# Feed-forward weights in 25 pieces, softmax by halves of heads in one-chain steps, and the first segment's sorted values copied tile to tile

## Chip, cores and metric

The kernel runs on one core of a Trainium2 chip. The metric is the device time of one execution in microseconds; smaller is better. The kernel before has a median of 1527.66 us over 3 runs (1521.85 to 1530.99).

## What is computed

x has 2048 rows of 448 numbers (bf16). Two kinds of layer alternate, A B A B, each added to its input:

```
x = x + A(layernorm(x));  x = x + B(layernorm(x));  x = x + A(layernorm(x));  x = x + B(layernorm(x))

A: mem = mem0                                     # 8 rows
   for each segment s of 32 rows (64 of them):
       h = concat(mem, x[s])                      # 40 rows
       q, k, v = h Wq, h Wk, h Wv                 # 16 heads of 256
       p = softmax(mask(q k^T / 16));  o = (p v) Wo
       mem = o[:8];  out[s] = o[8:]               # mem goes on to the next segment
B: ((gate * (gate > 0)) * up) W_down,  gate = x W_gate, up = x W_up      # 448 -> 1792 -> 448
```

The 64 segments of a layer A form a chain, since each needs the memory rows of the one before.

## The kernel before, in words

**Weights first.** The setup multiplies Wk with Wq per head into `M_sb`/`MT_sb`, and Wv with Wo into `B_sb`/`BT_sb` (lines 602 and 611), from transposed loads on SP's queue (line 584). So a segment needs no q, k or o of its own: scores are h M h^T, and "values" are h B, 448 wide for every head.

**69 steps.** The loop at line 706 runs steps g = 0 to 68. The first layer A is chain C1 (segments 0 to 63 in steps 0 to 63), the second is chain C2, five steps later (steps 5 to 68). Steps 0 to 4 hold C1 alone, steps 64 to 68 hold C2 alone (40 rows in use, "one-chain steps"); steps 5 to 63 hold both. The order on each engine is the order in which the Python code records it; nothing is moved afterwards. Each engine works in that order, and waits are on semaphores.

**One step** (`step`, line 451):

1. `project` (lines 396 to 439): G = h M, matmuls of lines 415 and 425, copied out of PSUM by ACT and DVE at line 435 (`G`, and the last slices into `GT`).
2. Scores `S_ps` (line 486), ten matmuls, two PSUM banks of eight heads each; all G matmuls of both banks come first, then those that need `GT`.
3. Softmax: maximum (line 492) and difference (494) on DVE, exp (496) on ACT.
4. `values` (line 302), 112 matmuls of line 314 into four banks `vps` in 14 slots of 8; the banks go to `VM` by line 332 after slots 10 and 13 (second bank on DVE, the others on ACT in the first chain). `between` is the rest of the softmax (lines 507, 508, 504: sum, reciprocal, `Px` for the 32 segment rows, `Pp` for the 8 memory rows), recorded behind the copies of slot 10. The matmuls of slots 8 and 11 wait for a no-op on SP that waits for the other row half's matmuls (lines 316 to 320), so what stands on SP's queue ahead of that no-op delays PE.
5. `PT`: the weights are transposed on PE (529, 532) and copied by ACT (530) and DVE (533).
6. `AT_ps` (545): the new rows, the memory rows among them; DVE and ACT copy these into `hTr` (552 to 554), and the next step's `project` begins.

At named places between these parts (G0, G4, G9, S, V, P, B, T), the plan of lines 710 to 779 puts other work: layer norms, feed-forward matmuls (`fill`), and `warm(8)`, eight matmuls without use (line 297), at V of steps 2 and 3.

**Values for four segments at once.** The first 8 rows of a segment's x make values `VX` by `first_values`, for four segments together (step 0, at V of step 1, and each fourth step). AT needs them sorted by head, `VP`. In general `pack` (line 355) writes VX to DRAM (`VD`) and reads it back sorted, two DMAs on SP. For the first four segments `pack_first` (line 360) uses 16 DMAs of 28 KB: segment 0 by four on ACT's queue (recorded ahead of step 0's `VM` copies), segments 1 to 3 by twelve on SP's.

**Feed-forward weights** come after setup has left their place free: `ffn_weights` (line 679) issues on SP at the end of step 0 four tiles of x in one DMA, W_gate (1344 KB) and its last 64 rows (224 KB); at the end of step 1 the same of W_up; at the end of step 2 W_down (1568 KB). They are first used in step 4. SP has no other work, so "at the end of a step" means behind the no-ops of that step's `values`.

**PSUM.** `bank()` hands out six banks in turn (line 75); a separate pair `ps2` holds one of the `gps`, then S_ps, then AT_ps.

Of the kernel before, what the change touches and what calls it, by code (L numbers as in the profile page):

```python
# [18 lines left out]
H = 16  # L19
# [6 lines left out]
F = 1792  # L26
# [17 lines left out]
def build_kernel(ctx, tc, A_x, A_mem0, A_Wq, A_Wk, A_Wv, A_Wo, B_W_gate, B_W_up, B_W_down, out,  # L44
# [30 lines left out]
    def bank(shape, dt, name):  # L75

        n_bank[0] += 1
        return psum.tile(shape, dt, tag=f"b{n_bank[0] % 6}", name=name)
# [207 lines left out]
    def fill(cid, n):  # L286

        for _ in range(n):
            if ffn_q[cid]:
                fn, a, b = ffn_q[cid].popleft()  # L290
                fn(a, b)
# [60 lines left out]
    p_dram = ctx.enter_context(tc.tile_pool(name="p_dram", bufs=1, space=bass.MemoryType.DRAM))  # L352
    VD = [p_dram.tile([4, P, DM], BF, name=f"VD{i}") for i in range(2)]

    def pack(c):

        nc.sync.dma_start(VD[c.cid][:, :, :].rearrange("g p d -> p g d"), VX[c.cid][:])
        nc.sync.dma_start(VP[c.cid][:], VD[c.cid][:, :, :].rearrange("g (q s) d -> (g q) s d", s=4))

    def pack_first(eng, segments):  # L360

        for k in segments:
            for g4 in range(4):
                eng.dma_start(VP[0][32 * g4:32 * g4 + 32, k, :], VX[0][k:P:4, g4, :])

    def score_tile(h, kind, m):
        return 28 * h + (7 * m + 3 if kind else 7 * (m // 6) + m % 6 + (m % 6 > 2))
# [83 lines left out]
    def step(g, plan):  # L451

        chains = [c for c in (C1, C2) if 0 <= g - c.lag < nseg]
        both = len(chains) == 2
        rg = g % NR
        c0, c1 = chains[0].cid, chains[-1].cid + 1
        NP = L * (c1 - c0)
        r_lo, r_hi = RB2 * c0, RB2 * (c1 - 1) + L
        RR = slice(r_lo, r_hi)
        nr = r_hi - r_lo  # L460
        hT = hTr[:, rg]

        def at_place(name):
            for f in plan.get(name, []):
                f()

        for _ in range(len(deferred)):
            deferred.popleft()()
        if g == 0:
            G = G_first  # L470
        else:
            G = p_vo.tile([P, 2, 24, 2, L], BF, tag="G", name="G")
            settle()
            project(G, hT, c0, c1, at_place)

        S_ps = psum.tile([P, 2, 512], F32, tag="ps2", name="S_ps")
        wide = {c.cid: RB2 if both and c is C1 else L for c in chains}
        for last in range(2):
            for bb in range(2):
                for c in chains:  # L480
                    w = wide[c.cid]
                    o = S_ps[c.rb:c.rb + w, bb, 0:8 * L]
                    o2 = o.rearrange("p (r e k) -> p r e k", e=2, k=L)
                    for sl in (3, 4) if last else (0, 1, 2):
                        rhs = GT[:, sl - 3, 4 * bb:4 * bb + 4, c.cid, :] if last else G[:, bb, sl:24:3, c.cid, :]
                        nc.tensor.matmul(o2[:, :, sl - 3, :] if last else o, hT[:, sl].rearrange("p c t -> p (c t)")[:, L * c.cid:L * c.cid + w], rhs,  # L486
                                         start=(sl == 0), stop=(sl > 2), tile_position=(0, c.rb),
                                         skip_group_check=True)

        S3 = S_ps[RR, :, 0:8 * L].rearrange("p b (h k) -> p b h k", k=L)  # L490
        mx = p_soft.tile([P, 2, 8], F32, tag="mx")
        nc.vector.tensor_reduce(mx[RR], S3, axis=AX.X, op=ALU.max)
        se = p_soft.tile([P, H, L], F32, tag="se")
        nc.vector.tensor_tensor(se[RR].rearrange("p (b h) k -> p b h k", b=2), S3,  # L494
                                mx[RR].unsqueeze(3).to_broadcast([nr, 2, 8, L]), op=ALU.subtract)
        nc.scalar.activation(se[RR], se[RR], AF.Exp, scale=SCALE)  # L496
        at_place("S")
        ssum = p_soft.tile([P, H], F32, tag="ssum")
        rs = p_soft.tile([P, H], F32, tag="rs")
        Px = p_soft.tile([P, H, SEG], BF, tag="Px")  # L500
        Pp = p_soft.tile([P, H, XB], BF, tag="Pp")

        def weigh(eng, dst, lo, hi):
            eng.tensor_tensor(dst, se[RR, :, lo:hi], rs[RR, :].unsqueeze(2).to_broadcast([nr, H, hi - lo]), op=ALU.mult)  # L504

        def weights():
            nc.vector.tensor_reduce(ssum[RR, :], se[RR], axis=AX.X, op=ALU.add)  # L507
            nc.vector.reciprocal(rs[RR, :], ssum[RR, :])  # L508
            weigh(nc.vector, Px[RR], XB, L)
            weigh(nc.gpsimd if both else nc.vector, Pp[RR], 0, XB)  # L510

        if g == 0:
            lean[0] = 4
            value_weights(weights)
            first_values(C1)
            pack_first(nc.scalar, (0,))
        for c in chains:
            first = c is chains[0]
            values(lambda rows, sl: hT[rows, sl, c.cid, XB:L], VM[c.cid], [cp_a, cp_v, cp_a, cp_a if first else cp_v],
                   weights if first and g else lambda: None)  # L520
            if first:
                at_place("V")
        if g == 0:
            pack_first(nc.sync, (1, 2, 3))

        PT = p_soft.tile([P, 5, RB2 + L], BF, tag="PT")
        PT_ps = bank([P, 4, P], BF, "PT_ps")
        for g4 in range(4):
            nc.tensor.transpose(PT_ps[:, g4, RR], Px[RR, 4 * g4:4 * g4 + 4, :], ident[RR, RR])  # L529
        cp_a(PT[:, 0:4, RR], PT_ps[:, :, RR])  # L530
        PP_ps = bank([P, P], BF, "PP_ps")
        nc.tensor.transpose(PP_ps[:, RR], Pp[RR, :, :], ident[RR, RR])
        cp_v(PT[:, 4, RR], PP_ps[:, RR])
        at_place("P")
        settle()

        at2 = psum.tile([P, 2, 512], F32, tag="ps2", name="AT_ps")
        at = at2[:, 0, 0:8 * L].rearrange("p (k c t) -> p k c t", c=2, t=L)
        order = (0, 1, 4, 2, 3)
        for k in order:  # L540
            for kd in range(4):
                lo = min(128 * kd, DM - 128)
                for c in chains:
                    w = VM[c.cid][:, k, :] if k < 4 else VP[c.cid][:, (g - c.lag) % 4, :]
                    nc.tensor.matmul(at[:, kd, c.cid, :], w[:, lo:lo + 128], PT[:, k, c.rb:c.rb + L],  # L545
                                     start=(k == order[0] and kd == 0 and c is chains[0]), stop=(k == order[-1]),
                                     skip_group_check=True)
        nxt = [c for c in chains if g + 1 - c.lag < nseg]
        if nxt:
            n = slice(nxt[0].cid, nxt[-1].cid + 1)  # L550
            dst = hTr[:, (g + 1) % NR, :, n, SEG:L]
            nc.vector.tensor_copy(dst[0:64, 3], at[64:128, 3, n, SEG:L])  # L552
            nc.scalar.copy(dst[64:128, 4], at[64:128, 3, n, SEG:L])
            nc.vector.tensor_copy(dst[:, 0:3], at[:, 0:3, n, SEG:L])
        for c in chains:
            j = (g - c.lag) % 4
            (cp_a if c is C1 else cp_v)(OT[c.cid][:, :, 32 * j:32 * j + 32], at[:, :, c.cid, 0:SEG])
        at_place("B")
        settle()
        at_place("T")  # L560
        if g < 3:
            ffn_weights(g)

    bp_cm = tc.tile_pool(name="bpre", bufs=1)
    bp = bp_cm.__enter__()
# [110 lines left out]
            if i == 0:  # L676
                load_vo(3)

    def ffn_weights(g):

        if g == 0:
            bp_cm.__exit__(None, None, None)
            pw = ctx.enter_context(tc.tile_pool(name="pw", bufs=1))
            Wg["pool"] = ctx.enter_context(tc.tile_pool(name="p_fb", bufs=2))
            Wg["main"] = pw.tile([P, 3, 2, F], BF, name="Wgu")
            Wg["tail"] = pw.tile([P, F], BF, name="WguT")
            if R > 2:
                nc.sync.dma_start(x_ring[:, 2:R, :], x_dram[256:R * 128].rearrange("(t p) d -> p t d", p=P))
        if g == 2:
            nc.sync.dma_start(Wd_sb[:], B_W_down.rearrange("(f p) d -> p f d", p=P))  # L690
        else:
            w = (B_W_gate, B_W_up)[g]
            nc.sync.dma_start(Wg["main"][:, :, g, :], w[0:384].rearrange("(k p) n -> p k n", p=P))
            nc.sync.dma_start(Wg["tail"][64 * g:64 * g + 64, :], w[384:448])

    mps = transposed(mem0n, MEM)
    nc.vector.tensor_copy(mem0T[:, 0:4], mps[:, 0:4, 0:MEM])
# [8 lines left out]
    for g in range(nsteps):  # L706
# [5 lines left out]

        def put(place, f):
            plan.setdefault(place, []).append(f)

        def norm_at(key, t, first, second, n=P):
            put(first, lambda: hold.__setitem__(key, Norm(xsl(t)[0:n], n)))
# [56 lines left out]
            put("G9", lambda: prep_x(C1, gb + 2, transposed(hold["c1"], P)))  # L774
        if r:
            if not LAG <= g < nseg:
                put("V", lambda: fill(1, 4 if r < 3 else 3) if ffn_q[1] else warm(8) if r > 1 or gb else None)
            for place, n in (("P", (2, 2, 1) if g > nseg else (2, 2, 4)), ("B", (0, 0, 2) if g > nseg else (2, 2, 2))):
                put(place, lambda n=n[r - 1]: fill(1, n))
        step(g, plan)  # L780
# [81 lines left out]
```

## Time and profile before

| | |
|---|---|
| median of 3 runs | 1527.66 us (1521.85 to 1530.99) |
| the profiled execution: time / span | 1520.82 us / 1519.0 us |
| busy, share of the span: PE, DVE, ACT, POOL | 98%, 61%, 42%, 7% |
| steps, from the chain of waits: 1 / 2 / 3 | 83.2 to 100.6 / to 116.0 / to 129.9 us |
| steps 65 to 68 begin | 1447.4, 1462.1, 1476.1, 1491.7 us |
| DMA queue q1 (the kernel's own) / q8 (instructions) | 51.96 MB / 5.44 MB in 332 packets |

The span runs from the first to the last instruction; the execution's time is 1.8 us longer. The chain of waits goes back from the last instruction, at each step to what released it: it says which work set the time. In it "issue" is time in which the engine waited for nothing that the profile shows. `SPq` and `ACTq` are the queues from which DMAs are issued; q1 carries those of SP, q10 those of ACT, and q8 has 16 KB packets, PE's instructions (256 of 64 bytes; 332 of them are the 85,000 of PE).

### The profile page before, as it was taken

The page shows a single profiled execution, that of the slowest core. Times are in us where ns is not written, and L with a number is a line of the kernel's source. Part 1 is how long each engine was busy: PE and PEld are TensorE (multiplying, and loading weights), DVE is VectorE, ACT ScalarE, POOL GpSimd, SP SyncE. Part 2 cuts the span into 40 slices and gives each one's busy share as a digit, 9 for nine tenths or more (in the row PEclk, how much of TensorE's full clock was granted, in tenths as well). Part 3 has the DMA queues.
Part 4 walks back from the last instruction along what each step waited for, and adds up shares of the span by engine and source line. Part 5 has one row for each costly group of instructions (what it writes and reads, how often), then busy time and mean ns, then how long its engine had stood idle before and what let it go on. Part 6 is the DMA issues. An engine that isn't in the chain of part 4 may idle for free.

```text
span 1519.0 us, 89892 instructions
## 1 busy us (share of the span) xinstructions
PE 1483.8 (98%) x42503; PEld 1170.9 (77%) x42503; DVE 924.0 (61%) x1892; ACT 634.7 (42%) x1411; POOL 112.2 (7%) x227
## 2 busy tenths in 40 slices
PE   7989999999999999999999999999999999999998
PEld 4567777878787887878788787878778787878776
DVE  6745556666566655656666666656666665556655
ACT  4633444434344443434444343434444343434333
POOL 1000001000000000000000000000000000000000
PEclk9999999999999999999999999999999999999999
DMA  9831000000000101000010100000010000000000
GB/s 197 198 118 64 28 28 29 28 31 19 30 20 27 35 28 34 28 31 7 28 35 28 34 28 31 19 30 20 28 35 28 31 28 31 5 28 31 4 31 9
DMA packets 77122, 57.84 MB, mean 38 GB/s; under 512 B 45512, under 2 KB 71888, under 8 KB 76752
## 3 DMA queue, kind: packets, MB, share of 16 engines
q1 hardware_dynamic: 76544, 51.96, 12.1%
q8 instruction: 332, 5.44, 1.5%
q14 instruction: 38, 0.31, 0.1%
q10 hardware_dynamic: 208, 0.12, 0.0%
HBM read 24.55 MB, written 16.06 MB: 27 GB/s over the span
## 4 chain that ended last, share of the span: by engine, by line
PE 96%; DVE 2%; issue 1%; ACT 1%; POOL 0%; DMA 0%; DVEq 0%; ACTq 0%; POOLq 0%
PE vps L314 29%; PE gps L425 27%; PE gu L224 7%; PE S_ps L486 6%; PE dps L264 6%; PE gps L415 5%; PE gu L252 4%; PE AT_ps L545 4%; PE wps L611 2%; PE wps L602 2%; PE PT_ps L529 1%; PE tps L144 1%; PE gu L244 1%; PE ops L447 1%; DVE ssum L507 0%
## 5 line engine op out<-in xcount | busy, mean ns | idle before, releaser
L425 PE MATMUL gps<-hTr,M_sb 128*128 128x80 bf16 (+1 forms) x11424 | 425.3, 200 | 2.4 <-issue 2.3
L425 PEld LDWEIGHTS <-M_sb 128*128 128x128 bf16 x11424 | 404.9, 100 | 11.0 <-issue 2.7
L314 PE MATMUL vps<-B_sb,hTr 64*32 64x448 bf16 x12288 | 355.6, 350 | 0.1
L314 PEld LDWEIGHTS <-hTr 64*32 64x32 bf16 x14336 | 204.0, 93 | 130.5 <-issue 8.7
L435 DVE CAST G<-gps 128x480 bf16<-128x480 f32 (+1 forms) x272 | 168.4, 619 | 187.2 <-PE gps L425 96.3
L435 ACT CAST G<-gps 128x480 bf16<-128x480 f32 (+1 forms) x272 | 144.6, 532 | 267.7 <-PE gps L425 261.8
L332 ACT CAST VM<-vps 128x448 bf16<-128x448 f32 x325 | 161.2, 531 | 144.5 <-PE vps L314 138.8
L332 DVE CAST VM<-vps 128x448 bf16<-128x448 f32 x187 | 113.4, 624 | 73.4 <-PE vps L314 73.4
L224 PE MATMUL gu<-xnT,Wgu 128*128 128x128 bf16 (+1 forms) x1548 | 125.2, 218 | 0.0
L496 ACT ACTIVATE se<-se 104x640 f32<-104x640 f32 (+1 forms) x69 | 50.9, 737 | 157.7 <-DVE se L494 157.7
L224 PE MATMUL gu<-xnT,WguT 128*128 128x128 bf16 (+2 forms) x516 | 111.3, 218 | 0.0
L224 PEld LDWEIGHTS <-Wgu 128*128 128x128 bf16 x1548 | 104.6, 98 | 1.7 <-issue 1.5
L504 POOL TENSOR_TENSOR Pp<-se,rs 104x128 bf16<-104x128 f32 x59 | 48.1, 816 | 732.2 <-DVE rs L508 698.2
L314 PE MATMUL vps<-BT_sb,hTr 64*32 64x448 bf16 x2048 | 96.9, 349 | 0.2 <-issue 0.2
L415 PE MATMUL gps<-hTr,MT_sb 64*128 64x80 bf16 (+1 forms) x3808 | 91.5, 197 | 4.7 <-DVE hTr L552 3.1
L314 PE MATMUL vps<-B_sb,hX 64*32 64x448 bf16 x3072 | 89.8, 350 | 4.8 <-DVE hX L153 2.6
L264 PE MATMUL dps<-Wd_sb,hh 128*128 128x448 bf16 (+1 forms) x448 | 90.7, 353 | 0.0
L415 PEld LDWEIGHTS <-MT_sb 64*128 64x128 bf16 x3808 | 74.0, 97 | 20.6 <-issue 9.7
L230 DVE SCALAR_TENSOR_TENSOR hh<-gu,ut 128x256 bf16<-128x256 f32 (+1 forms) x129 | 53.7, 418 | 53.0 <-ACT ut L229 48.9
L314 PEld LDWEIGHTS <-hX 64*32 64x32 bf16 x3584 | 52.6, 92 | 36.8 <-issue 5.2
L486 PEld LDWEIGHTS <-hTr 128*40 128x40 bf16 (+1 forms) x1280 | 66.2, 104 | 18.6 <-issue 0.3
L545 PE MATMUL AT_ps<-PT,VM 128*128 128x40 bf16 x2048 | 72.4, 179 | 6.6 <-ACT PT L530 6.6
(108 smaller groups left out, 1684.6 us busy)
## 6 DMA issues: line engine op xcount, KB each, us to landing
VD<-VX SPq DMA_DIRECT2D x31, 448.0 KB, 3.1
VP<-VD SPq DMA_DIRECT2D x31, 448.0 KB, 3.1
wvo<-in_A_Wo_dram SPq DMA_DIRECT2D x2, 896.0 KB, 6.1
out_dram<-x_ring SPq DMA_DIRECT2D x15, 112.0 KB, 2.1
Wd_sb<-in_B_W_down_dram SPq DMA_DIRECT2D x1, 1568.0 KB
x_ring<-in_A_x_dram SPq DMA_DIRECT2D x12, 112.0 KB, 2.2
Wgu<-in_B_W_gate_dram SPq DMA_DIRECT2D x1, 1344.0 KB, 7.6
Wgu<-in_B_W_up_dram SPq DMA_DIRECT2D x1, 1344.0 KB, 6.3
```

The source lines that it names most:

```text
L224: nc.tensor.matmul(ps[:, i, ff], w, self.xnT[:, kd if kd < 3 else 3 + i], start=(kd == 0), stop=(kd == 3))
L230: nc.vector.scalar_tensor_tensor(out=self.hh[:, f:f + 2, :], in0=ps[:, 0], scalar=0.0, in1=ut[:, 0:2, 0:self.n], op0=ALU.max, op1=ALU.mult)
L252: nc.tensor.matmul(ps[i][:, ff], Wg["main"][:, kd, i, (f + ff) * 128:(f + ff) * 128 + 128], self.xnT[:, kd], start=False, stop=(kd == 2), ...
L264: nc.tensor.matmul(self.dps[0:self.n, 0:DM], self.hh[:, f, :], Wd_sb[:, f, :], start=(f == 0), stop=(f == FT - 1))
L314: mm = nc.tensor.matmul(ps[g4][32 * hq:32 * hq + 32, 0:DM], lhsT(rows, i if i < 3 else 3 + r), w, start=first, stop=final, tile_position=( ...
L332: evac[g4](dst[:, g4, :], ps[g4][:, 0:DM])
L415: nc.tensor.matmul(ps[h, b][:, i * NP:(i + 1) * NP], MT_sb[rows, t * 128:(t + 1) * 128], hT[rows, 3 + h, c0:c1, :], start=(i == 0), stop=F ...
L425: nc.tensor.matmul(ps[h, b][:, i * NP:(i + 1) * NP], M_sb[:, kd, t * 128:(t + 1) * 128], hT[:, kd, c0:c1, :], start=False, stop=(kd == 2), ...
L435: cp(o, src)
L486: nc.tensor.matmul(o2[:, :, sl - 3, :] if last else o, hT[:, sl].rearrange("p c t -> p (c t)")[:, L * c.cid:L * c.cid + w], rhs, start=(sl ...
L496: nc.scalar.activation(se[RR], se[RR], AF.Exp, scale=SCALE)
L545: nc.tensor.matmul(at[:, kd, c.cid, :], w[:, lo:lo + 128], PT[:, k, c.rb:c.rb + L], start=(k == order[0] and kd == 0 and c is chains[0]), ...
```

## The change

1. **Weights in pieces.** x tiles 2 to 5 one by one, W_gate and W_up in six pieces and one tail each (229 KB), W_down in seven: 25 DMAs in a list. Two are issued at the end of step 0, and one at each of the eight places of steps 1, 2 and 3. All stay on SP's queue.
2. **Softmax by halves** in one-chain steps other than 0, 4 and 64, so in steps 1, 2, 3, 65, 66, 67, 68. Each half of eight heads has a bank of its own from `bank()`, its scores are completed (GT matmuls too) before the other half's begin, and maximum, difference, exp, sum, reciprocal and Px are done for each half. All of it is recorded ahead of `values`, so ahead of the copy of the second `vps` bank on DVE. Pp moves to POOL, by halves. PT goes in two parts: heads 0 to 7 by ACT; heads 8 to 15 and the memory rows by DVE; AT takes the memory rows last.
3. **Segment 0's sorted values** go by two DMAs on ACT's queue and two on POOL's; segments 1 to 3 by `pack` instead of twelve small DMAs.
4. `warm(5)` for `warm(8)`.

```
-    def pack_first(eng, segments):
-        for k in segments:
-            for g4 in range(4):
-                eng.dma_start(VP[0][32 * g4:32 * g4 + 32, k, :], VX[0][k:P:4, g4, :])
+    def pack_first():
+        for g4, eng in enumerate((nc.scalar, nc.gpsimd, nc.scalar, nc.gpsimd)):
+            eng.dma_start(VP[0][32 * g4:32 * g4 + 32, 0, :], VX[0][0:P:4, g4, :])
...
+        halves = not both and g > 0 and (g % 4 > 0 or g > nseg)
+        if halves:
+            S_b = [bank([P, 512], F32, "S_ps")[:] for bb in range(2)]
...
-        for last in range(2):
-            for bb in range(2):
+        for last, bb in ((0, 0), (1, 0), (0, 1), (1, 1)) if halves else ((0, 0), (0, 1), (1, 0), (1, 1)):
...
+        if halves:
+            hs = [slice(8 * bb, 8 * bb + 8) for bb in range(2)]
+            for bb in range(2):
+                Sh = S_b[bb][RR, 0:8 * L].rearrange("p (h k) -> p h k", k=L)
+                nc.vector.tensor_reduce(mx[RR, bb], Sh, axis=AX.X, op=ALU.max)
+                nc.vector.tensor_tensor(se[RR, hs[bb]], Sh, mx[RR, bb].unsqueeze(2).to_broadcast([nr, 8, L]),
+                                        op=ALU.subtract)
+                nc.scalar.activation(se[RR, hs[bb]], se[RR, hs[bb]], AF.Exp, scale=SCALE)
+            for bb in range(2):
+                weights(hs[bb])
...
-                   weights if first and g else lambda: None)
+                   weights if first and g and not halves else lambda: None)
...
-            pack_first(nc.sync, (1, 2, 3))
+            pack(C1, 1)
...
+        n1 = 2 if halves else 4
+        for lo, hi, cp in ((0, n1, cp_a), (n1, 5, cp_v)):
+            PT_ps = bank([P, hi - lo, P], BF, "PT_ps")
+            for k in range(lo, hi):
+                Pk = Px[RR, 4 * k:4 * k + 4, :] if k < 4 else Pp[RR, :, :]
+                nc.tensor.transpose(PT_ps[:, k - lo, RR], Pk, ident[RR, RR])
+            cp(PT[:, lo:hi, RR], PT_ps[:, :, RR])
...
-        order = (0, 1, 4, 2, 3)
+        order = (0, 1, 2, 3, 4) if halves else (0, 1, 4, 2, 3)
...
+        for t in range(2, R):
+            loads.append((x_ring[:, t, :], x_dram[t * 128:(t + 1) * 128, :]))
+        half = F // 2
+        for i, w in enumerate((B_W_gate, B_W_up)):
+            for kd in range(3):
+                for c in (slice(0, half), slice(half, F)):
+                    loads.append((Wg["main"][:, kd, i, c], w[kd * 128:kd * 128 + 128, c]))
+            loads.append((Wg["tail"][64 * i:64 * i + 64, :], w[384:448]))
+        wd = B_W_down.rearrange("(f p) d -> p f d", p=P)
+        for f in range(0, FT, 2):
+            loads.append((Wd_sb[:, f:f + 2], wd[:, f:f + 2]))
+        load_some(2)
...
+        if 0 < g < 4:
+            for place in ("G0", "G4", "G9", "S", "V", "P", "B", "T"):
+                put(place, load_some)
...
-                put("V", lambda: fill(1, 4 if r < 3 else 3) if ffn_q[1] else warm(8) if r > 1 or gb else None)
+                put("V", lambda: fill(1, 4 if r < 3 else 3) if ffn_q[1] else warm(5) if r > 1 or gb else None)
```

## The prediction

> **What bounds the kernel now.** I read first the page's chain of waits (its shares by engine), then the chain in order of time, to see where PE is not the link, then what SP's queue and the DMA queues did at those places.
>
> ```profile
> PE 96%; DVE 2%; issue 1%; ACT 1%; POOL 0%; DMA 0%; DVEq 0%; ACTq 0%; POOLq 0%
> ```
>
> PE sets the time nearly everywhere. The change leaves steps 4 to 64 (129.9 to 1447.4 us) as they are, so it can touch only the 4% and only in steps 0 to 3 and 65 to 68. The chain in order of time (start, length, work), step 1 to step 2 and then the softmax of step 3:
>
> ```profile
> 90.81 4.47 PE vps L314 x183
> 95.28 2.24 issue
> 97.52 1.31 PE vps L314 x41
> ...
> 102.25 1.22 issue
> ...
> 125.86 0.63 DVE VM L332
> 126.48 0.73 DVE ssum L507
> 127.23 0.26 DVE rs L508
> 127.51 0.69 DVE Px L504
> 128.26 0.28 PE PT_ps L529 x4
> 128.61 0.30 ACT PT L530
> 128.96 0.70 PE AT_ps L545 x20
> ```
>
> Two holes of 2.24 and 1.22 us in which PE waits for nothing that is shown; and in step 3 a stretch that DVE ends. For the holes, the issues on SP (start, length), then the queues in 91.8 to 94.9 us and in 94.9 to 95.3 us:
>
> ```profile
> 79.18 8.41 SPq L364 DMA_DIRECT2D VP<-VX  x12
> 87.64 0.59 SPq L688 DMA_DIRECT2D x_ring<-in_A_x_dram  x1
> 88.33 0.45 SPq L693 DMA_DIRECT2D Wgu<-in_B_W_gate_dram  x1
> 88.82 1.62 SPq L694 DMA_DIRECT2D WguT<-in_B_W_gate_dram  x1
> 95.23 0.37 SPq L693 DMA_DIRECT2D Wgu<-in_B_W_up_dram  x1
> 95.64 0.99 SPq L694 DMA_DIRECT2D WguT<-in_B_W_up_dram  x1
> ```
> ```profile
> q1 hardware_dynamic: 351, 1.18, 100.0%
> ```
> ```profile
> q1 hardware_dynamic: 12, 0.02, 20.8%
> q8 instruction: 1, 0.02, 19.6%
> ```
>
> (Packets, MB, share of 16 engines.) In the first window q1, full of W_gate, has everything and q8 nothing; in the second, as the burst runs dry, one 16 KB page of instructions starts, at 94.97. It takes 1.25 us, and PE goes on 1.3 us after it has landed, at 97.52. The next page starts at 100.86 as W_up runs dry, takes 1.30, and PE goes on at 103.47, again 1.3 later. PE crosses a page of 256 instructions in about 3.1 us (values) to 3.5 us (project), and asks for the next at the crossing, here about 92.1 and 97.5. An undisturbed page takes some 0.3 + 1.2 + 1.3 = 2.8 us and is just in time; 2 to 3 us behind a burst is a hole.
>
> **The change, part by part.**
>
> *Step 0, sorted values.* ACT is held by four issues of 28 KB (77.47 to 80.59, 0.78 us each), so its three VM copies run from 80.63 to 82.03, PT's copy behind them, and AT starts at 82.28. Two issues end at 79.03; the first VM copy goes at 79.55, the last two must await the end of values (80.15): VM done at 81.3, PT 81.6, AT 81.7: **-0.5**. POOL's two DMAs have no row. From below, ACT's price: issued by 79.0, landed 2.8 later at 81.8 (AT's third group needs it at 81.95: no cost). From above, one after the other at 2.8 each from 77.4: 83.0, AT ends 0.5 later than before. I take -0.5, nearest to ACT's row of the same DMA, and keep +0.5. pack's two DMAs (3.1 us landing each) are issued at 79.2 and 82.3 and land at 85.4; step 1's AT needs them at 98: hidden.
>
> *The pieces on SP.* None has a tie to PE other than its place among SP's no-ops, so SP runs ahead and they go in groups: four x tiles and two gate pieces at 82.7 to 85.3 (A); one behind step 1's values; **seven**, 1.6 MB, behind first_values of step 1 (C); eight, 1.8 MB, behind step 2's values (D); three in step 3. An issue takes 0.37 to 0.45 us by the W_gate, W_up and W_down rows, a piece drains in 0.57 us (229 KB at the 400 KB/us of W_gate). No no-op waits: C ends 3 us after its start, the next no-op is needed 12 us later.
>
> *First hole.* W_gate no longer stands in the queue at 92; only one piece does (0.57 us). The page lands in time, and the 41 matmuls that took 1.31 run at the 0.024 us of the 71 ahead: first_values would end at 96.06 instead of 98.81, **-2.75**.
>
> *A new wait in step 1.* Banks go round by six: two for S, four for values, so the fourth bank of first_values is that of the second vps bank, whose VM copy stands on DVE behind the whole halved softmax. A DVE instruction is 0.155 us + 1/960 us for each element (0.82 for 640, 0.69 for 512, 0.28 for 128), so the halves are: maximum, difference 0.49 each, sum 0.48, reciprocal 0.23, Px 0.42; twice that with gaps of 0.03 is 4.5 us from the first maximum to the last Px, against 4.54 now. The first maximum starts 0.4 earlier (90.4 in step 1), the last Px ends at 94.8, VM at 95.5. PE reaches slot 4 of first_values at 94.3 and stands until 95.5, **+1.25**; the halved scores add 0.1 (PE waits for GT of the first half). What is behind on PE is the rest of first_values and AT; ACT's VX copies wait for it too. First_values ends at 97.4, not 98.8: with the first hole, step 1 gives **-1.4**. Softmax itself is hidden there.
>
> *Second hole.* The page in question is asked for at the crossing in slot 9 of first_values, C issued behind slot 7. C's data begin 1.0 us after its first issue (W_down: issued 111.51, data from 112.5), and a quarter of the 332 pages in the trace start even before the array is at the crossing: the page goes ahead of C, and the next is needed only after C has drained. **-1.2**. Of the other groups, A is issued slower than its 112 KB tiles drain (0.3 us), so the page of 84 us finds gaps; D drains by 117.4, and softmax keeps PE from the next crossing until then (117.8 now): nothing from either.
>
> *Steps 2 and 3.* Px ends 0.46 earlier in step 3. Behind it DVE does VM (0.62) and PT's second part (0.28), then 12 of AT's 20 matmuls remain (0.42): 1.35 us to AT's end instead of 1.5. Pp on POOL has no row at 64 elements: between 0.22 (rstd) and 0.82 (Pp, 128 elements), I take 0.52, halfway in elements too; by either end DVE's VM covers all but 0.1 of it. warm(5) ends at 127.5, ahead of Px. **-0.45** in step 3; in step 2 the maximum also waits for DVE's copy of hTr, **-0.3**.
>
> *Steps 65 to 68.* PE has feed-forward matmuls at V and P. PT waited 0.1, 0.1, 0.25 and 0.54 us for Px; the halved scores cost 0.1 each where no transposes stand ahead, and PT's second bank waits for the late VM copy in steps 67 and 68. **-0.1** in all.
>
> Sum: -0.5 - 1.4 - 1.2 - 0.3 - 0.45 - 0.1 = **-3.95 us**: 1520.82 becomes 1516.9. The profiled execution lies 6.8 below the median of the runs shown, so I carry the difference to the median: **1523.7 us**, 0.26% less. A measurement of this kernel tells about 0.5% (7.6 us) from no change, so this is "within".
>
> **Rivals.**
>
> *The page waits for C after all.* If it is not ahead of C, C's data run from 96.85 for 4.0 us and the page gives PE back 2.6 later, at 103.45, where it was at 103.47 before: steps 0 and 1 gain nothing, 0.85 is left: 1526.8. For it: both bursts above held a page to their last packet. Against: both had been issued in full when the page was asked for. The Trainium skill ("DMA: Bandwidth & Descriptors", Queues, rings and completion order) says that each DMA engine goes round-robin between queues at packet granularity; by that no page waits for a burst, and this rival falls. The 3.1 us with nothing in q8 speak against the rule.
>
> *Slower: pieces that drain slowly, with the page behind all of them.* PE comes back at 96.85 + 7p + 2.6 for a piece of p us; with 0.85 gained elsewhere, this is slower than before from p = 0.7. Group A could also hold a page that project needs at 87.5, 1.8 us. At p = 1.0: back at 108.2, +3.9: 1531.6; if pieces went singly at the landing time of 112 KB and 448 KB (2.2 and 3.1 us, so about 2.5), +10 and more. Against: W_gate, its tail and x were in flight together at 400 KB/us. The Trainium skill ("DMA: Bandwidth & Descriptors", Measured) asks for DMAs of 1 MiB or more, with 0.95 us for 64 KB and 6.15 for 1 MB; between these, an estimate of 1.8 us a piece, it gives this rival. No run here has a piece of that size; at 1568 KB the trace's 400 KB/us is above the 341 GB/s given there for 1 MB.
>
> *Faster: the clock.* PE's granted clock is 0.88 to 0.90 in steps 1 to 3 and 1.00 in steps 65 to 67, by the windows view; step 3's 96 matmuls of L425 take 2.86 against 2.53 there. If fewer holes let the clock up, up to 0.7 a step: some 2 us more, 1521.7. Against: the idle stretches around AT remain.
>
> **How the numbers follow.** Forecast 0.57 (1523.7); page behind C 0.20 (1526.8); clock 0.13 (1521.7); slow pieces 0.10 (1531.6 and up). The range leaves out most of the last and allows for the scatter of the runs, which differ by 9 us among themselves: 1517 to 1530. The first three cases lie within 0.5%, the scatter puts some of the forecast and the clock case beyond it: faster 0.11; of the slow pieces those with p above 1.5: slower 0.06; within 0.83.
>
> **What would show it.** Right: no "issue" piece over 0.5 us between 90 and 104; an idle of 1.2 us on PE in first_values of step 1, ended by DVE's VM; AT of step 0 at 81.7; step 3 in 13.4 us instead of 13.9; SP's issues in groups of 6, 1, 7, 8, 3. Wrong: a hole near 100 that ends when q1 runs dry; a wait for POOL's DMA in step 0; any difference after 130 and before 1447 us.

## The result, and the profile after

The kernel after has a median of **1519.68 us** over 22 runs (1513.61 to 1523.95); the kernel before, run beside it, 1523.51 over 22 (1520.78 to 1530.99). The ratio of the runs is 0.9968, 95% interval 0.9956 to 0.9979: 4.9 us less (3.2 to 6.7); the two medians lie 3.8 us apart. Forecast were 3.95 less and 1523.7. The level is 4 us off because the median of the 3 runs before, 1527.66, was itself 4 above that of the 22. Of the runs below, one execution of the pieces alone, the profiled one, took 2069.32 us at a granted clock of 0.654, and the ratios leave it out.

The two profiled executions do not show the gain at all: span 1519.0 us before, 1519.8 after. So the stages have to be compared. First the shares of the chain of waits of the kernel after, the same line of the page as was shown of before:

```profile
PE 95%; DVE 1%; SPq 1%; issue 1%; DMA 1%; ACT 1%; POOL 0%; DVEq 0%; ACTq 0%
```

A DMA has 1% now, where it had 0% before, and SP's queue is new in it. Next the chain in order of time (start, length, work), steps 1 to 3 of after:

```profile
87.62 1.23 issue
...
96.32 0.62 DVE VM L332
96.94 0.04 issue
96.98 2.10 PE vps L314 x76
...
105.43 1.60 issue
107.03 1.02 PE gps L424 x34
...
119.53 1.64 issue
...
126.13 1.05 PE warm L297 x5
127.19 0.24 PE PT_ps L549 x5
```

Three holes, 4.47 us in all, where before had two of 3.46. The one in first_values is gone; a new one is in step 1's project, the one in step 2's project is still there, and step 3's project has one too. `PT` in step 3 no longer waits for DVE: warm(5) ends it.

Where the second hole comes from is told by SP's queue (timeline, 95 to 106 us) and by the DMA queues in 102.4 to 104.5 and in 104.5 to 104.9 us (packets, MB, share of 16 engines):

```profile
98.02 1.28 SPq L701 DMA_DIRECT2D Wgu<-in_B_W_gate_dram  x3
99.34 0.89 SPq L701 DMA_DIRECT2D WguT<-in_B_W_gate_dram  x1
100.28 1.53 SPq L701 DMA_DIRECT2D Wgu<-in_B_W_up_dram  x3
```
```profile
q1 hardware_dynamic: 335, 0.57, 101.9%
```
```profile
q1 hardware_dynamic: 74, 0.12, 81.6%
q8 instruction: 1, 0.02, 17.2%
```

These seven are group C. PE crosses into a new page of 256 instructions at about 102.3 (counted back from 107.03) and asks for the next; for 2.1 us q1 has every engine and q8 nothing; the page starts at 104.56, as C runs dry, and PE goes on 2.5 us later. One page (at 98.96) did go ahead of C; the next one met its end. C drained at 258 KB/us (1.55 MB from 98.9 to 104.9 us), so 0.89 us a piece. The Trainium skill ("DMA: Bandwidth & Descriptors", Queues, rings and completion order) lets a DMA engine change queues after each packet, and counts some 9 to 17 descriptors as one packet, 64 at most. The 335 packets of q1 here are single rows of mostly 1792 bytes, 21 for each of 16 engines. If a row is what the skill calls a descriptor, a wait of that length is within its bound of 64. So this trace does not refute the rule, though the prediction took the like for a refutation; nor does any run here show that the rule is the cause.

That the holes are pages of instructions can be told from all the traces. Between 83 and 140 us the thirteen traces used here have 37 stretches of 0.27 us and more in which PE stands and waits for nothing that is shown. Each ends at the same place in PE's count of matmuls and weight loads (193 above a multiple of 256), and 2.2 to 2.8 us after a 16 KB page has started.

The stages of twelve executions that are used below, in us, from the marks in the chains: when the first values matmul of step 0 starts; the lengths of steps 0 to 3 from there; step 4; steps 5 to 63; and from there to the end.

| execution | setup ends | 0 | 1 | 2 | 3 | sum 0 to 3 | 4 | 5 to 63 | rest |
|---|---|---|---|---|---|---|---|---|---|
| before | 74.47 | 8.93 | 17.35 | 15.47 | 13.87 | 55.61 | 22.63 | 1268.2 | 98.11 |
| after | 75.21 | 8.58 | 17.11 | 14.01 | 13.89 | 53.58 | 21.72 | 1272.8 | 96.44 |
| again (after, 2nd time) | 77.60 | 8.07 | 17.05 | 12.70 | 13.36 | 51.17 | 21.72 | 1270.8 | 97.04 |
| pieces_look | 75.40 | 8.97 | 15.95 | 14.91 | 13.95 | 53.78 | 22.64 | 1267.5 | 98.16 |
| halves_only | 74.56 | 9.27 | 18.43 | 15.25 | 12.73 | 55.69 | 22.31 | 1271.0 | 96.88 |
| sorted_only | 74.63 | 8.67 | 19.06 | 14.64 | 13.83 | 56.19 | 22.62 | 1268.6 | 98.68 |
| paced | 76.61 | 8.44 | 14.72 | 13.57 | 12.53 | 49.26 | 22.67 | 1272.4 | 97.02 |
| paced_only | 75.67 | 9.23 | 15.43 | 14.27 | 13.47 | 52.40 | 22.71 | 1272.0 | 98.43 |
| pace_act | 74.19 | 8.62 | 15.32 | 12.48 | 12.81 | 49.23 | 23.20 | 1269.1 | 97.19 |
| pace_nowarm | 75.09 | 8.38 | 15.50 | 12.73 | 12.71 | 49.33 | 22.59 | 1270.3 | 96.61 |
| nowarm | 74.44 | 8.34 | 15.52 | 12.92 | 13.92 | 50.70 | 22.62 | 1269.5 | 96.20 |
| nopool | 75.05 | 8.41 | 16.16 | 13.91 | 15.47 | 53.95 | 22.04 | 1267.3 | 96.92 |

What no edit touches differs too: setup by 3.4 us, steps 5 to 63 by 5.5. (`Rest` holds step 64 too, which is 25.98 us before and 25.97 after.) That is why two profiles of equal length can hide a gain of 4. One column does split: the rest is 98.1 to 98.7 us in the four kernels without the halved softmax, and 96.2 to 97.2 in the eight with it.

### The profile page after: what moved, and what is told of

It is laid out like the page before. It is cut to its first block, busy times and chain, and to the rows that moved or that the text cites. A ratio compares the mean times of both kernels' runs of the same rounds, so it can differ in the third digit from the quotient of the medians.

```text
span 1519.8 us, 89950 instructions
## 1 busy us (share of the span) xinstructions
PE 1483.1 (98%) x42497; PEld 1167.3 (77%) x42497; DVE 926.9 (61%) x1920; ACT 636.1 (42%) x1418; POOL 120.2 (8%) x243
## 4 chain that ended last, share of the span: by engine, by line
PE 95%; DVE 1%; SPq 1%; issue 1%; DMA 1%; ACT 1%; POOL 0%; DVEq 0%; ACTq 0%
PE vps L314 28%; PE gps L424 27%; PE gu L224 7%; PE dps L264 6%; PE S_ps L489 6%; PE gps L414 5%; PE gu L252 4%; PE AT_ps L562 4%; PE wps L619 2%; PE wps L628 1%; PE PT_ps L549 1%; PE tps L144 1%; SPq L601 1%; PE gu L244 1%; DMA B_sb<-in_A_Wq_dram 1%
## 5 line engine op out<-in xcount | busy, mean ns | idle before, releaser
L503 POOL TENSOR_TENSOR Pp<-se,rs 104x128 bf16<-104x128 f32 (+1 forms) x73 | 54.8, 750 | 809.0 <-DVE rs L508 761.8
L527 ACT ACTIVATE se<-se 104x640 f32<-104x640 f32 (+1 forms) x62 | 45.7, 737 | 140.8 <-DVE se L525 140.8
```

Of the source, the lines that this page charges most:

```text
L503: eng.tensor_tensor(dst[RR, hs], se[RR, hs, lo:hi], rs[RR, hs].unsqueeze(2).to_broadcast([nr, n, hi - lo]), op=ALU.mult)
```

## The experiments

My theory: a group of pieces holds one page of PE's instructions until it has drained, so the 25 pieces move the holes and do not remove them; the gain comes from the halved softmax, from the clock, and from steps 65 to 68. The rival: the pieces do the work, and what holes are left are PE's own and not DMA's.

### One part at a time

Three kernels, each the kernel before with one part of the change: the pieces (`loads`, `load_some`, the eight places), the halves (`halves`, with Pp on POOL, PT in two parts and `warm(5)`), the sorted values (`pack_first` and `pack(C1, 1)`).

> The kernel before with the 25 pieces alone. Theory (groups): SP sends the pieces in groups, as it did in the changed kernel, and each group holds one page of PE's instructions; the sum of the 'issue' holes between 83 and 125 us stays at 3.5 to 5 us (3.46 before, 4.47 in the changed kernel), step 4 begins within 1 us of where it did (129.9 us), ratio 0.999 to 1.001. Rival (the prediction): the holes go, step 4 begins 2.5 to 3 us earlier, ratio 0.998.

> The kernel before with the softmax by halves and warm(5) alone. Theory (groups): most of the gain is here, about 1 us in steps 1 to 3, 1.5 us in steps 65 to 68, and what fewer half-clock windows give: 2.5 to 3.5 us, ratio 0.998. The two holes of the kernel before stay, the first of them beside the new wait for the VM copy. Rival (the prediction): 0.75 us in steps 2 and 3, 0.1 in steps 65 to 68, and 1.25 lost in step 1: ratio 1.000.

> The kernel before with the first segment's values tile to tile and pack for the other three alone. Theory (POOL's transfer is late): AT of step 0 waits for DMA VP in its third group and ends 0.3 to 0.5 us later than before; the burst of W_gate comes earlier, since twelve issues are gone from SP, so its hole moves into step 1's project with about the same length; ratio 1.000 to 1.001. Rival (the prediction): AT ends 0.5 us earlier, ratio 0.9997.

| alone | median, us | ratio to before | interval |
|---|---|---|---|
| pieces | 1522.72 (11 runs) | 0.998 | 0.996 to 1.0 |
| halves | 1521.81 (12) | 0.9985 | 0.9977 to 0.9994 |
| sorted values | 1522.98 (12) | 0.9999 | 0.9988 to 1.001 |

Only the halves alone are told from no change by their interval: 2.3 us less (0.9 to 3.5), a little under what my theory asked for. In halves_only the rest behind step 63 is 96.88 against 98.11, and step 3 is 12.73 against 13.87, but step 1 is longer: its hole in first_values is still there (2.47 us), and PE stands 0.46 us ahead of it for DVE's VM. The interval of the pieces holds both the theory's number and the rival's. Sorted_only met neither expectation: AT does wait for the DMA, 0.7 us, yet step 0 is 0.26 shorter, and its first hole (2.35; the second is 1.24) is in step 1's values, not in project. Step 1 is 1.71 longer, with a second half-speed window in it, from 94.4 us.

The pieces alone once more, for their trace:

> The kernel before with nothing but the 25 pieces (softmax whole, sorted values and warm(8) as before). Theory (each group of pieces holds one page of PE's instructions, and the pieces only move the holes): the two holes of before, 2.24 and 1.22 us, are replaced by two or three holes of 1.2 to 1.7 us in steps 1 and 2, 3.0 to 4.7 us in all, each ending 1.2 to 1.4 us after a 16 KB page that started as q1 ran dry; steps 1 to 3 together 46.0 to 47.5 us long (before 46.7; whole change 45.0). Rival (the pieces do take holes away, and the holes of the whole change come from its other parts, the halves with their own banks and the shifted softmax): holes under 1.5 us in all, steps 1 to 3 44.5 us or less.

1521.35 us, ratio 0.999 (0.9977 to 1.0004). Two holes, 0.83 and 1.39 us, 2.2 in all against 3.46, and steps 1 to 3 take 44.81 against 46.69. That lies between the two expectations: the pieces by themselves take a third of the idle time away, not none. The hole in step 2's project, 1.39 us, stands where the whole change has its 1.60.

### Each piece tied to PE

The whole change, with a no-op in front of each piece that waits for PE's latest matmul, so that SP can't run ahead:

```
 def load_some(n=1):
     for _ in range(min(n, len(loads))):
         dst, src = loads.popleft()
+        if last_pe:
+            tie = nc.sync.nop(hint="piece")
+            after(tie, last_pe[-1])
         nc.sync.dma_start(dst, src)
```

> The changed kernel, with each piece behind a no-op on SP that waits for PE's latest matmul at the piece's place, so that the 25 go out one by one over steps 1 to 3. Theory (groups): at most one or two pieces are in the queue when a page is asked for; no hole over 0.6 us between 84 and 125 us, where the changed kernel has 1.23, 1.60 and 1.64; step 4 begins 3 to 4 us earlier than in the changed kernel; ratio to before 0.994 to 0.995. Rival (the holes are PE's own, not the queue's): holes of the same sum, ratio 0.997 as for the changed kernel.

1516.46 us (6 runs), ratio 0.9951 (0.9934 to 0.9967). SP's queue (timeline, 85 to 127 us), where the six W_gate pieces are now spread over 9.7 us, instead of going two, one and three:

```profile
90.53 9.68 SPq L709 DMA_DIRECT2D Wgu<-in_B_W_gate_dram  x6
...
102.48 10.88 SPq L709 DMA_DIRECT2D Wgu<-in_B_W_up_dram  x6
...
114.88 11.00 SPq L709 DMA_DIRECT2D Wd_sb<-in_B_W_down_dram  x7
```

and in the chain of paced, step 1 has no hole, step 2 one of 0.34 us (at 105.11) and step 3 one of 0.29.

Steps 1 to 3 take 40.82 us, 4.2 less than after, of which 3.8 are the holes. The holes are made by DMAs in a group: same work, same bytes, only spread. The rival falls. But a part of the gain is lost again in step 4, which has a hole of 0.78 us that after has not and is 0.95 longer: its page started at 129.21, behind the last pieces and the first DMA of `pack`. Steps 1 to 4 together are 3.2 us shorter, as the median is, and the intervals of paced and of after still overlap.

### The same spreading without the rest of the change

> The kernel before with the 25 pieces alone, each behind a no-op on SP that waits for PE's latest matmul, so that they come one at a time over steps 1 to 3; softmax whole, sorted values and warm(8) as before. Theory (a group of pieces holds a page, a single piece does not): no hole over 0.5 us in steps 1 to 3, where before has 2.24 and 1.22; steps 1 to 3 together 42.5 to 44 us (before 46.7, pieces without pacing 44.8), ratio 0.996 to 0.998. Rival (pacing helps only together with the halves): holes of 1 us and more stay, ratio as that of the pieces without pacing, 0.998 to 1.0.

The kernel before with paced pieces alone: 1522.74 us (11 runs), ratio 0.9991 (0.9976 to 1.0005). Steps 1 to 3 take 43.17, inside what was expected, but holes of 0.59 and 0.84 us stay (and another of 0.84 in step 4) where none over 0.5 was expected, and the ratio missed. In this execution steps 5 to 63 took 1272.0 against 1268.2. So the expectation for the stage held and that for the whole did not; I can't show that pacing alone gains anything.

### The whole change a second time

> The whole change once more, nothing altered. Theory (a profiled execution differs from another of the same program in setup, where PE waits 0 to 2 us for a transposed load of Wq at 21 to 23 us, and in how long each hole is, since the pieces have no tie to PE): the first values matmul of step 0 starts at another time than 75.21, by up to 1.5 us; the holes come at the same places (in project of step 1, in project of steps 2 and 3) with sizes that differ by up to 1 us from 1.23, 1.60 and 1.64; steps 0 to 3 together 51 to 54.5 us (53.58 in the first profile). Rival (the program decides, and the profile of the whole change can be compared with that of before to 0.2 us): every one of these within 0.2 us of the first profile.

1521.01 us (11 runs), ratio 0.998 (0.997 to 0.999). The rival falls, but the scatter is larger than my theory allowed: setup ends 2.4 us later (up to 1.5 was expected), and the three holes are 1.23, 0.29 and 1.11 where they were 1.23, 1.60 and 1.64 (up to 1 apart was expected). In setup PE waits for loads of weights (line, what it waited for, us, times, longest; 20 to 24 us):

```profile
PE wps L628 <- DMA B_sb<-in_A_Wq_dram: 1.7, 1, 1.7
```

1.7 us here, 1.3 in the first profile of after, 2.0 in paced, 0.7 in nowarm, none in before. That is 0.4 of the 2.4 us; the second profile also has two waits for `wvo`'s loads, 2.3 us, which the first has not. A program, run twice, differs by more in this and in the holes than most terms of my sum. The hole at 1.23 in step 1 is there both times.

### The route of the sorted values

```
-        for g4, eng in enumerate((nc.scalar, nc.gpsimd, nc.scalar, nc.gpsimd)):
+        for g4, eng in enumerate((nc.scalar, nc.sync, nc.scalar, nc.sync)):
```

> The whole change, with the two DMAs of segment 0's sorted values that went by POOL's queue on SP's queue instead (ACT, SP, ACT, SP). Theory (POOL's route is what costs step 0 its 0.39 us: its DMAs take 3.6 us from issue to landing): AT of step 0 no longer waits for VP, its first matmul starts at about 82.0 and its last ends at about 82.9; step 0 ends 0.5 to 0.8 us earlier, at 83.0 to 83.3 where it was 83.79. Rival (28 KB within SBUF take this long by any queue, or SP's two issues of about 0.7 us each delay the no-op for which PE waits in values): a wait of AT for VP, or an idle of PE in values, of at least 0.4 us stays, and step 0 ends at 83.6 or later. The median moves by less than 0.1% by either.

1516.96 us (5 runs), ratio 0.996 (0.994 to 0.998). As expected, the ratio is within 0.001 of after's. AT still waits for a DMA, 0.3 us instead of 0.6, and step 0 ends at 83.46, between the two expectations. The DMAs by SP's queue land after 2.7 us and those by POOL's after 3.8 in after, but after 2.7 in paced and 2.6 in nowarm, by POOL as well. So POOL's route as the cause falls; the landing time of 28 KB scatters between 2.0 and 4.1 us by POOL's queue, 1.8 and 3.9 by ACT's, 1.8 and 3.5 by SP's. Why isn't shown; the 448 KB of `pack` are issued behind them each time.

### Whole rows

W_gate and W_up in three pieces each instead of six (rows of 3584 bytes, 458 KB):

```
-                for c in (slice(0, half), slice(half, F)):
+                for c in (slice(0, F),):
```

> The whole change, with W_gate and W_up in three pieces of whole rows (458 KB, rows of 3584 bytes) instead of six of half rows (229 KB, 1792 bytes), so 19 DMAs. If the size of the rows sets the drain (1792 B took 74 ns in the median and 98 in the mean, 3584 B 140): q1 moves 360 to 390 KB/us in the groups of W_gate and W_up, as before, against 231 to 270 in the whole change. If each DMA costs a fixed 0.25 to 0.3 us: about 310 to 335 KB/us. If it is the issue rate on SP (one in 0.4 to 0.5 us): 229 KB pieces can't exceed 460 to 570 KB/us, so that would have been no limit. By all of them the holes stay in number, since the pieces still go in groups, and are between 1 and 2.5 us each.

One run, 1520.85 us. None of the three was right: W_up's rows of 3584 bytes drained at 265 to 305 KB/us (0.53 MB in 98 to 100 us, 0.61 in 100 to 102), not 370 or more, and less than a fixed cost for each DMA gives. So the row length isn't what sets the drain, and why W_gate in one DMA moved 381 KB/us before (1.18 MB in 3.1 us) stays open. The holes changed in number, too. One stands out, 4.45 us at 103.71, in step 2's project. Here the page started between 105.5 and 106, behind all that was queued. This is the case that I had priced as the slow pieces.

### Without the warm matmuls

```
-  put("V", lambda: fill(1, 4 if r < 3 else 3) if ffn_q[1] else warm(5) if r > 1 or gb else None)
+  put("V", lambda: fill(1, 4 if r < 3 else 3) if ffn_q[1] else None)
```

> The whole change without its warm(5) at V of steps 2 and 3, so PE does nothing while it waits for the softmax there. Theory (the granted clock falls to half for 3.41 us when PE was too little in use in the stretch before, and the whole change has only one such window in steps 1 to 3 where before had three): half-speed windows return in steps 3 and 4, two or more between 100 and 155 us; the 72 matmuls of project behind them take 2.2 us instead of 1.91 or the 96 take 2.86 instead of 2.5; steps 3 and 4 together 0.6 to 1.4 us longer than the whole change's 35.6. Rival (the windows follow the stretch around AT, whatever stands at V): windows where the whole change has them, steps 3 and 4 within 0.3 us.

1515.83 us (7 runs), ratio 0.9956 (0.994 to 0.9971). In this execution the stage went as the theory has it; windows of before (steps 2 and 3), of after (1, 2, 3) and of nowarm (step 3), with stretch, length, busy us of PE, PEld, DVE, ACT, POOL, granted clock, DMA share and GB/s:

```profile
100.75:116.21 15.46, 13.40 (x384) 10.38 (x383) 8.34 (x20) 5.04 (x14) 1.34 (x3) 0.89 0.27 77
116.21:130.08 13.87, 13.04 (x380) 10.14 (x379) 6.89 (x17) 4.79 (x13) 0.00 (x0) 0.88 0.23 76
```
```profile
83.79:100.90 17.11, 14.69 (x484) 11.27 (x483) 8.35 (x23) 6.06 (x16) 0.89 (x2) 0.90 0.43 119
100.90:114.90 14.00, 11.93 (x380) 9.26 (x380) 8.45 (x24) 5.35 (x15) 1.69 (x4) 1.00 0.46 128
114.90:128.79 13.89, 11.68 (x377) 9.06 (x376) 7.13 (x20) 5.09 (x14) 1.38 (x3) 1.00 0.49 140
```
```profile
111.22:125.14 13.92, 11.80 (x371) 9.62 (x371) 7.12 (x20) 5.00 (x14) 1.38 (x3) 0.88 0.44 123
```

The clock of steps 2 and 3 is 0.89 and 0.88 before, 1.00 and 1.00 after, and 0.88 again in step 3 without the warm matmuls. Steps 3 and 4 take 36.54 us against 35.61, 0.93 more. But warm matmuls alone don't keep the clock: nopool has `warm(5)` too, and half-speed windows in steps 2 and 3 (from 100.9 and 121.4 us, granted clock 0.88 and 0.89). Between 115 and 140 us it is the only one of the seven executions with halves and `warm(5)` that has such a window; without `warm(5)` both executions have one. Up to V of step 2 this program is the same as after; that its step 1 took 15.52 against 17.11 (a hole of 0.37 for 1.23, and full clock) is scatter. Its ratio is no better than after's as far as the intervals tell.

The same in the paced version:

> The paced version of the whole change without warm(5) at V of steps 2 and 3. Theory (PE too little in use around the softmax brings half-speed windows, as in the whole change without warm(5), where steps 3 and 4 were 0.93 us longer): two or three half-speed windows between 100 and 150 us, steps 1 to 4 together 0 to 1.5 us longer than paced's 63.5, ratio 0.995 to 0.997. Rival (with the holes gone PE is in use enough, and the warm matmuls only keep PT's transposes waiting): at most one window there, steps 2 and 3 0.1 to 0.4 us shorter each, ratio 0.994 to 0.995.

1515.67 us (5 runs), ratio 0.9945 (0.9931 to 0.9958). Three half-speed windows (from 112.2, 125.9 and 146.3 us), as the theory said, but steps 1 to 4 take 63.5 us, as paced's do. Steps 2 and 3 are 0.66 us shorter together, since PT goes as soon as Px is there (Px ends at 122.83, PT's transposes start at 122.88); step 1, which is the same program in both, is 0.78 longer. So the clock theory holds for the windows, and in paced's steps the missing warm matmuls give back what they cost.

### The second VM bank on ACT

The paced version with segment 0's copies by ACT and SP, and

```
-  [cp_a, cp_v, cp_a, cp_a if first else cp_v]
+  [cp_a, cp_a if halves else cp_v, cp_a, cp_a if first else cp_v]
```

> The paced version of the whole change, with the two POOL issues of segment 0's sorted values on SP, and in the steps of the halves the second bank of VM copied by ACT instead of DVE. Theory (DVE's copy of that bank stands behind the halved softmax, so first_values waits 0.38 to 0.46 us in step 1, and PT's second part waits for it on DVE): the wait of first_values for DVE's VM goes; step 1 0.4 us shorter than paced's 14.73, steps 2 and 3 shorter by 0 to 0.3 each, steps 65 to 68 by 0 to 0.3 each; ratio 0.9935 to 0.995. Rival (ACT is as late: its copy stands behind exp and holds back PT's first part): step 1 and the softmax steps unchanged or up to 0.3 longer each, ratio 0.995 to 0.9965.

1516.28 us (6 runs), ratio 0.9953 (0.9938 to 0.9968). The wait of first_values for DVE's VM is gone from the chain, but in step 2 ACT's VM copies (107.51 to 109.20 us) now stand on the chain ahead of PT's copy, and step 1, with a half-speed window from 84.0 us, took 15.32 and not the 14.3 expected. Steps 1 to 3 are 40.61 against 40.82: no difference that can be told. The rival was nearer.

Pace_act and pace_nowarm ran on one chip with the repeat of after: 1514.65 to 1519.91 and 1513.94 to 1517.40 against 1519.78 to 1524.21. So these two are about 5 us faster than the change itself on that chip. That it is the pacing isn't shown: each has another edit besides, nowarm and nopool, without pacing, are at 1515.83 and 1516.96, and pace_act's holes from step 1 to step 4 sum to 2.1 us, as nowarm's do (2.0). Among all of these no order is shown.

## Why the prediction was right, point by point

It was right in sign and size (3.95 forecast, 4.9 measured, 3.2 to 6.7), but several of its terms were wrong, and they cancelled: that the total came so near is in good part luck. What was right in kind, and made the gain, is the halved softmax, at four times the size forecast. Measured are after and again against before, counted from the end of setup:

| step of the sum | forecast | after | again |
|---|---|---|---|
| step 0 | -0.5 | -0.35 | -0.86 |
| step 1 | -1.4 | -0.24 | -0.30 |
| step 2 (second hole, softmax) | -1.5 | -1.46 | -2.77 |
| step 3 | -0.45 | +0.02 | -0.51 |
| step 4 | 0 | -0.91 | -0.91 |
| steps 65 to 68, with the end | -0.1 | -1.67 | -1.07 |
| sum | -3.95 | -4.61 | -6.42 |

*Step 0: about right.* A wait for POOL's DMA of sorted values came, 0.6 us in after, which the prediction had named as a sign of being wrong. Counted from the end of setup, the last of the four landed 0.3 us behind the sum's lower bound, 81.8, and 0.9 ahead of the upper one.

*The pieces' groups: right.* SP issued 6, 1, 7, 8 and 3.

*First hole: gone, as said. Group A: wrong.* "The page of 84 us finds gaps" failed: in after it started at 86.58, and the hole was 1.23 us in both profiles. This is most of what is missing in step 1, and was in the prediction as a part of a rival (1.8 us).

*The new wait in step 1: right in kind, mis-sized.* 0.38 us and not 1.25: from the first maximum to VM's start the halved chain took 4.0 us (92.33 to 96.32) instead of 4.5 from the first maximum to the last Px.

*Softmax of steps 2 and 3: right in kind, mis-sized.* From the last scores matmul to the last of AT no hole and, in these executions, no window intervenes. Step 3 of before, then of after (chains):

```profile
122.41 1.20 PE S_ps L486 x10
...
128.96 0.70 PE AT_ps L545 x20
```
```profile
122.10 1.26 PE S_ps L489 x10
...
127.70 0.67 PE AT_ps L562 x20
```

So 6.05 us became 5.01, and step 2 has 6.0 and 5.0 as well: 1.04 less in each, where 0.3 and 0.45 were forecast. The step that failed is the length of the halved chain: from the first maximum to the last Px it takes 4.13 us in step 3 (122.87 to 127.00) and not 4.5, since a DVE instruction can start before the one ahead of it has ended (the second maximum starts at 123.86, the difference ahead of it runs from 123.45 to 123.93), where the sum had gaps of 0.03. Against the end of the scores, the first maximum starts 0.53 us earlier than before, for a forecast of 0.4. What stands behind Px went as forecast, 1.37 us for 1.35; only `warm(5)` ends 0.19 us after Px and not ahead of it. The stretch is 6.0 to 6.1 us in steps 2 and 3 of all four kernels without halves; with them and `warm(5)` it is 5.0 in all seven, but for 6.2 in nopool's step 3 and 5.5 in whole_rows' step 2, which ran in part at half speed; without `warm(5)` it is 4.8 to 4.9.

*Second hole: wrong.* "The next is needed only after C has drained" is the step that failed. C drained in 0.89 us a piece, not 0.57, and the hole was 1.60 and 0.29 us in the two executions, 1.22 before. The page did go ahead of C; it was the next page that met C's end, which neither my forecast nor my rival had. The quarter of the pages that start ahead of their crossing is too many as well: counted by 256 instructions from the first hole of before, it is 26 of 332.

*Group D: wrong.* "D drains by 117.4", ahead of the crossing at 117.8, failed in the same way: step 3 began 1.3 us earlier than before, PE crossed at about 116.4, D was in the queue until 119, the page started at 118.94, and step 3's project has a hole of 1.64 us (1.11 in the second profile). It ate what step 3 gained by softmax and clock.

*What made up for it, beside the softmax.* The clock, given 0.13: steps 2 and 3 at 1.00 instead of 0.89 and 0.88, and step 4 0.91 shorter. By the 72 matmuls of project, 1.91 us at full clock and 2.2 with a half-speed window, and the 96, 2.5 and 2.86, such a window costs about 0.7 us there. In after one fell on step 5 instead (1.63 us longer), in again none did.

*Steps 65 to 68: right in kind, mis-sized most.* I had taken the waits of PT for Px as 0.1 to 0.54 us and let costs eat them. Step 67 of before, then of after (chains, start, length, work):

```profile
1485.52 0.62 DVE VM L332
...
1487.31 0.70 DVE Px L504
...
1488.06 0.27 PE PT_ps L529 x4
```
```profile
1484.79 2.77 PE vps L314 x112
1487.56 1.00 PE gu L224 x16
1488.56 0.76 PE dps L264 x4
1489.32 0.22 PE PT_ps L549 x5
```

Before, DVE's chain from VM to Px decides when PT starts; after, PE never leaves the chain there, and the step is 0.62 us shorter. From the last scores matmul to the last of AT the four steps are 0.29, 0.29, 0.42 and 0.46 us shorter, 1.46 in all. These four lengths are the same, within 0.01 us, in all four kernels without halves and in all nine with them, but for pace_act's step 68. Of the costs that I had set against it, PT's second part does wait for the late VM copy in step 68 (VM from 1503.40 to 1504.03, PT at 1504.08); the step is shorter all the same.

*"Any difference after 130 and before 1447 us" came, and is not settled.* Steps 5 to 63 run the same program in all kernels, yet took 1267.3 to 1272.8 us. The jumps, up to 1.6 us, lie mostly in steps 5, 13, 17, 21 and so on, which have first_values and pack's DMAs; the two executions of after differ by 2.0 there, 1.63 of it the half-speed window in step 5.

*The other signs.* Of those of being right, the groups on SP came, and no hole lies between 90 and 104 us; but holes of 1.23 and 1.60 us lie just outside, at 87.62 and 105.43. PE's wait for VM was 0.38 us and not 1.2. AT of step 0 started at 82.0, or 81.2 counted from before's end of setup, ahead of the 81.7 forecast, but then stood 0.6 us for the DMA. Step 3 took 13.89 us and not 13.4 (13.36 in the second profile).

## What to carry to other kernels

Cutting a transfer into pieces doesn't spread it: pieces with no tie to the work run ahead in a group and hold the instruction pages as the whole did; put a wait in front of each. In steps 1 to 3 of the four paced traces that left holes of 0.4 to 1.7 us in all, where the five with the same pieces untied have 2.0 to 4.5; what it gives in the median isn't shown by itself. Look for which page meets the end of which group, not only whether one page gets ahead. And compare two profiles by stages from a common mark, with the same program profiled twice, before a term under 1 us is believed. Better still is a stretch that nothing else touches: from the last scores matmul to the last of AT, the halved softmax is worth the same 1.04 us in every undisturbed execution, while the totals scatter by several us.

## What the runs showed of the hardware

- **The clock falls on a raster.** Half-speed windows last 3.41 us or a whole multiple (10.24 us in halves_only from 100.7, 6.83 in whole_rows from 106.2), and in each execution their starts differ by multiples of that: before 83.4, 103.9, 117.5 and 131.2 (6, 4 and 4 times 3.41 apart), after 88.9 and 150.3 (18), pace_nowarm 84.9, 112.2, 125.9 and 146.3 (8, 4 and 6). So where a window falls relative to a step is chance. The Trainium skill ("TensorE: Matmul & The Clock Gate", What's actually happening) describes a free-running activity window of this length, and these starts agree. The same page's advice (Why this matters for your kernels) is to avoid idle gaps of PE over some 3 us; to keep to it isn't enough here, since the longest idle of PE in the 10 us ahead of after's window at 88.9 was 1.23 us. What exactly tips it is not shown: the holes of 1.60 and 1.64 us in after brought none.
- **Short DMAs in a row drained slower than one long one**: 258 KB/us in pieces of 229 KB (group C), 265 to 305 in pieces of 458 KB, 381 in the middle of one DMA of 1344 KB (328 over that whole burst, 2.04 MB from 88.8 to 95.0 us). The cause is open.
- **A page of PE's instructions waits behind a queued burst.** In the 37 holes counted above, PE goes on 2.2 to 2.8 us after its page has started; the page of 102.3 us started 2.2 us late, as the 335 packets of q1 ran out.
